# Transformer layer on one core: idle products behind the last products with v, the projection's column blocks in order 2, 3, 0, 1, and the paced DMA list served twice a unit

## The chip, the cores and the metric

The kernel runs on one core of a Trainium2 chip. The core has TensorE (PE in the profile; its weight loads are listed apart as PEld), VectorE (DVE), ScalarE (ACT), GpSimd (POOL) and SyncE (SP). Here SP's queue issues all the DMAs that matter. The metric is the device time of one execution in microseconds, lower being better.

## The reference

The layer normalises its input and adds an attention block and a feed-forward block to it:

```python
xn = layernorm(x)                      # x: 2048 x 512, float32
q, k, v = split(xn @ wqkv)             # 32 heads of 16
p = softmax(q @ k.T * 16 ** -0.5)      # per head 2048 x 2048
a = (p @ v) @ wo
h = gelu(xn @ w1 + b1) @ w2 + b2       # 512 -> 1792 -> 512
out = x + a + h
```

The kernel holds most float32 operands as a pair of float16 (high part and rest) and forms a product from three terms: high x high, high x rest, rest x high.

## The kernel before

**Units.** The heads are taken four at a time (8 groups g), the queries in 4 blocks of 512 (qb). A pair (g, qb) is a turn t, of which there are 32; a turn has 16 units, so there are 512. Unit u forms, for four heads, the scores whose row maxima are wanted (`s_half`: PE, then a maximum on DVE, L363). For the unit 19 before it (`LEAD`) it forms the transposed scores with the maximum taken off and their exponentials (`e_half`: PE, then ACT, L411), and for the units 20 and 21 before it the products with v (`v_half`), two halves a unit. A product uses 64 rows of the array and 32 columns; so PE runs two halves side by side, and beside each half of products with v it runs "dense" products on the other 64 rows, from a generator of groups: first the rest of v and the projections of q and k, then the feed-forward block, at last the output projection. `dense` takes 3 or 4 products of a group for each half.

**Order of the work.** Every engine's instructions are issued in the order in which the program writes them. `later(n, fn)` runs a function n slots on, a slot being the end of a unit (`tick`). A function with a size (`bulk`, in KB) is not run when it is due but goes to the end of the paced list (`lane`), from which `run_due` takes items while its credit is positive; the credit is raised by `LANE` once a unit and lowered by the item's size, and what is left of it is not kept. In the tick before every sixteenth unit the list is held (`held`), so that the store of a turn's maxima (L394) in that unit's first half goes ahead.

**First phase (`ph1`).** On the list are the stores of the normalised input (L1174), the loads of the weights for splitting (L812, `chunk`), the stores of the split weights (L1241, L1243), the stores of projected q and k (L592, L593) and the loads of the next group's q and k rows (`stacks`, L507). The weights for q and k come in four blocks of 128 columns; `load_qk(m + 1)` (L560) is called four slots after block m is split, and issues two loads of 256 KB directly. `split_qk` splits them with ACT (L149) and POOL (L151, L152), by the time project(m) begins; two buffers hold the loaded columns.

**After a turn.** `v_end` copies the four heads' sums from PSUM (L437). Through DRAM the sums of the exponentials are turned, inverted on DVE and spread over 128 partitions (`spread`, L463, four DMAs of 64 KB). POOL multiplies and splits, and L474 stores the turn's rows of the output projection's input (`ot_d`), after which the turn is in `ready`. For the last turn `last_one` does this on the chip instead: transposes on PE (L489), reciprocal and product on DVE (L491, L492), transposes back (L495), then the high part on ACT (L497) and the rest on DVE (L498).

**Tail.** `tail` yields the output projection's groups, by column block qb: 12 products on the lower 64 rows of the array and 12 on the upper. Blocks 2 and 3 are begun "early": they leave out the last 64 input rows (group 7's heads), which follow as `o_end` groups of three products on one side. `fetch(qb, n)` asks for a block's input (`oc`, L1361) n slots on. `when` lets it go once its turn is in `ready` and the unit number is in 4 to 13 of a sixteen, or past 512. The four pieces of the read and the reads of the accumulators (L1365) are on the list; `known` says that a block has been read. Block 3 needs turn 27, blocks 0 and 1 need turns 28 and 29, and the last rows of block 2 turn 30. Past unit 512 there are no scores, and `spare` puts products of a second group in their places, four a unit. `finish` adds the scaled product to the accumulator (L1371, DVE) and stores the result (L1368).

Of the kernel before, what the change touches and what calls it, by code (L numbers as in the profile page):

```python
# [36 lines left out]
WARM = 430  # L37
NV = 11
LAG, E_TAIL = 3000, 8000
LANE = 420  # L40
WFROM, WSTEP, XN = 10, 4.5, 4.5
VT = 2600, -2000
WV_TAIL, WV_DVE = 50000, 2
# [11 lines left out]
def layer_kernel(ctx: ExitStack, tc: tile.TileContext, x, wqkv, wo, w1, b1, w2, b2, out):  # L55
# [51 lines left out]
    def banks(tag):  # L107
        k = free_banks[tag].pop(0)
        free_banks[tag].append(k)
        return bank_tile(k, tag)  # L110
# [37 lines left out]
    def split_pool(hi, lo, src, inv):  # L148
        nc.scalar.activation(hi, src, AF.Copy, scale=inv)  # L149
        given("act", 1000)  # L150
        nc.gpsimd.tensor_scalar(src, src, inv, 0.0, op0=ALU.mult, op1=ALU.add)  # L151
        nc.gpsimd.tensor_tensor(lo, src, hi, op=ALU.subtract)  # L152
# [138 lines left out]
    def run_due(all_of_them=False):  # L291
        due = sorted((q for q in queue if q[0] <= slot[0]), key=lambda q: q[0])
        queue[:] = [q for q in queue if q[0] > slot[0]]
        for q in due:
            if q[3]:
                lane.append((q[3], q[1]))
            else:
                q[1]()
        credit[0] = min(credit[0], 0) + LANE
        while lane and (all_of_them or credit[0] > 0 and not held[0]):  # L300
            size, fn = lane.pop(0)
            credit[0] -= size
            fn()
# [123 lines left out]
    def v_end(u):  # L427

        t, kt = divmod(u, 16)
        g, qb = divmod(t, NQB)  # L430
        for h in range(4):
            del ptiles[u, h]
        if kt < 15:
            return
        pv, k = pv_of.pop(t)
        osb = work.tile([P, QB], F32, name="osb", bufs=2)
        nc.scalar.activation(osb, pv, AF.Copy)  # L437
        given("act", 600)
        free_banks["S"].append(k[0])
        if t == NG * NQB - 1:  # L440
            later(0, lambda: last_one(osb))
            return

        dn = work.tile([64, 32], F32, name="dn", bufs=1)
        rb = work.tile([P, QB], F32, name="rb", bufs=1)

        def sums():
            for h in range(4):
                nc.sync.dma_start(den_d[t, 0, h:h + 1, :], osb[32 * h + DH:32 * h + DH + 1, :])

        def turned():
            nc.sync.dma_start(dn, den_d[t, 0].rearrange("h (c q) -> (h c) q", q=32))

        def inverse():
            nc.vector.reciprocal(dn, dn)
            given("dve", 330)

        def keep():
            nc.sync.dma_start(den_d[t, 1].rearrange("h (c q) -> (h c) q", q=32), dn)

        def spread():
            for h in range(4):
                nc.sync.dma_start(rb[32 * h:32 * h + 32, :], den_d[t, 1, h:h + 1, :].to_broadcast([32, QB]))  # L463

        def store():
            ot = work.tile([P, 2, QB], F16, name="ot", bufs=2)
            pooled((1280, lambda: nc.gpsimd.tensor_tensor(osb, osb, rb, op=ALU.mult)),  # L467
                   (620, lambda: nc.gpsimd.tensor_scalar(ot[:, 0], osb, 1.0, 0.0, op0=ALU.mult, op1=ALU.add)),
                   (1160, lambda: nc.gpsimd.tensor_tensor(ot[:, 1], osb, ot[:, 0], op=ALU.subtract)),
                   (0, lambda: later(6 if t < (NG - 1) * NQB else 1, put)))  # L470

            def put():
                for h in range(4):
                    nc.sync.dma_start(ot_d[64 * g + DH * h:64 * g + DH * h + DH, :, qb * QB:(qb + 1) * QB],  # L474
                                      ot[32 * h:32 * h + DH])
                ready.add(t)


        at = (1, 3, 6, 7, 9, 12) if t < (NG - 1) * NQB else (1, 2, 5, 6, 7, 8)
        for k, fn in zip(at, (sums, turned, inverse, keep, spread, store)):  # L480
            later(k, fn)

    def last_one(osb):

        on = work.tile([P, 4, 4, DH], F32, name="on")
        rden = work.tile([P, 4, 4], F32, name="rden")
        pq = banks("S")
        for q in range(4):
            nc.tensor.transpose(pq[:, q * P:(q + 1) * P], osb[:, q * P:(q + 1) * P], ident)  # L489
        pqv = pq.rearrange("p (q h e) -> p q h e", q=4, h=4)  # L490
        nc.vector.reciprocal(rden, pqv[:, :, :, DH])  # L491
        nc.vector.tensor_tensor(on, pqv[:, :, :, 0:DH], rden.unsqueeze(3).to_broadcast([P, 4, 4, DH]), op=ALU.mult)  # L492
        pt = banks("S")
        for q in range(4):
            nc.tensor.transpose(pt[:64, q * P:(q + 1) * P], on[:, q].rearrange("p h d -> p (h d)"), ident)  # L495
        ot = work.tile([P, 2, QB], F16, name="ot", bufs=2)
        nc.scalar.activation(ot[:64, 0], pt[:64, :], AF.Copy)  # L497
        nc.vector.tensor_tensor(ot[:64, 1], pt[:64, :], ot[:64, 0], op=ALU.subtract)  # L498
        last.append(ot)
# [18 lines left out]
    class Group:  # L518
# [32 lines left out]
        def end(self):  # L551
            self.finish(self.bank)
            if self.key is not None:
                free_banks[self.key[1]].append(self.key[0])

    def load_qk(m):
        wf = []
        for w in range(2):
            wf.append(ph.tile([P, D], F32, name="wq", bufs=2).rearrange("p (c n) -> p c n", n=P))
            nc.sync.dma_start(wf[w], wqkv[:, w * D + m * P:w * D + (m + 1) * P].rearrange("(c p) n -> p c n", p=P))  # L560
        return wf

    def split_qk(m, wf, inv, ready_w):
        wh = ph.tile([P, 2, 2, NC, P], F16, name="wqk_h", bufs=2)
        for w in (1, 0):
            split_pool(wh[:, w, 0], wh[:, w, 1], wf[w], inv[:, 8 + 2 * min(m, 2) + w:9 + 2 * min(m, 2) + w])
            yield
        ready_w[m] = wh
        if m < 3:
            later(4, lambda: wfs.append(load_qk(m + 1)), True)  # L570
# [175 lines left out]
    def unit(gen):  # L746


        u = pos[0]
        e = u - LEAD  # L750
        if e > 0 and e % (2 * NQB * 16) == 0 and e < NU:
            fetch_scale(e // (2 * NQB * 16))
        pos[0] += 1
        for a in range(2):
            for kind, b in ((1, 1), (0, 0), (0, 1), (1, 0)) if a == 0 else ((1, 2), (0, 3), (0, 2), (1, 3)):
                if kind and 0 <= e < NU:
                    e_half(e, b)
                elif not kind and u < NU:
                    s_half(u, b)
                elif not kind and u > NU:  # L760
                    spare(gen, b % 2)
            if e >= 0:
                one_more()
                enter()

                w, r = (e - 2, 1) if a == 0 else (e - 1, 0)
                live = 0 <= w < NU
                new = r == 0 and w % 16 == 0
                if live and not new:
                    v_half(w, r)  # L770
                dense(gen, 1 - r)
                if live and new:
                    v_half(w, r)

                for user, goes_on in (("V", live and not (r == 1 and w % 16 == 15)),
                                      ("D", cur[0] is not None and not cur[0].over())):
                    leave(user, goes_on)
                for k in backlog:
                    backlog[k] = max(0, backlog[k] - HALF)
                if live and r == 1:  # L780
                    v_end(w)
                ended(False)

            if a == 0 and u % 16 == 0 and u // 16 - 1 in stores:
                stores.pop(u // 16 - 1)()
        if u < NU:
            s_end(u)
        tick()
# [626 lines left out]
    with ExitStack() as st3:  # L1415
# [17 lines left out]
                    later(n + 1 + k % 4, lambda k=k: read_acc(acs[k], k))  # L1433

        def tail():
            for n, qb in enumerate((2, 0, 3, 1)):
                fetch(qb, (2, 4, 10, 16)[n])
            later(9, lambda: nc.sync.dma_start(wo_l, wo_s[64:128, :, NC - 1, :]))
            ends = set()

            def rows():
                nc.sync.dma_start(ol, ot_d[D - 64:, :, 2 * QB:3 * QB])
                ends.add(2)

            when((NG - 1) * NQB + 2, rows)
            for qb in (2, 0, 3, 1):
                while qb not in known:
                    yield None
                for q in range(4):
                    yield o_proj(qb, q, qb >= 2)  # L1450
            while not ends:
                yield None
            for q in range(4):
                yield o_end(2, q, ol)
            while not last:
                yield None
            for q in range(4):
                yield o_end(3, q, last[0])
# [37 lines left out]
```

## Time and profile before

| | |
|---|---|
| median of 3 runs | 1469.63 us (1469.29 to 1471.78) |
| profiled execution | 1469.13 us |
| its span, first to last instruction | 1467.4 us |
| mean granted TensorE clock | 0.997 |
| busy: PE, DVE, ACT, POOL | 99%, 93%, 86%, 45% |
| data moved | 124.86 MB, 85 GB/s on average |

The span is the time from the first to the last instruction of the profiled execution; its own time is 1.7 us more. A chain of work is followed backwards from the last instruction to whatever released it, so its shares say what the span was made of. "Idle before" is the time for which an engine stood still ahead of an instruction, with what ended it; "issue" means that nothing in the profile explains the wait. A window's row gives its limits and its length, the busy time and count of what was asked for, the granted TensorE clock, the busy share of the DMA engines and GB/s. In a timeline the first number is the start and the second the length, in us from the start of the span.

### The profile page before, as it was taken

To read this page: it belongs to the slowest core of one execution; us is meant where nothing else is said; L and a number is where in the kernel's file an instruction comes from. 1 tells how busy PE (TensorE), PEld (TensorE's weight loads), DVE (VectorE), ACT (ScalarE), POOL (GpSimd) and SP (SyncE) were. 2 spreads that over 40 slices of the span, in tenths; PEclk is the share of its full clock that TensorE was granted. 3 is DMA by queue.
4 is the path that set the end of the run, shared out by engine and by line. 5 is a ranking of instruction groups with operands and counts; after the bars stand their busy time and mean duration, and the time that the engine had idled before them with its cause. 6 is when DMAs were issued, how large, how long until landed. Compare 5 with 4: busy or idle time off the path is not lost.

```text
span 1467.4 us, 88634 instructions
## 1 busy us (share of the span) xinstructions
PE 1451.0 (99%) x40158; PEld 839.5 (57%) x40158; DVE 1369.4 (93%) x2305; ACT 1258.4 (86%) x2366; POOL 663.9 (45%) x672
## 2 busy tenths in 40 slices
PE   8999999999999999999999999999999999999998
PEld 4446565665566555556565556565555656555554
DVE  7989999999999999999999999999999999999933
ACT  5868888888999888899988889998889998888884
POOL 3201957663778401288831138883115787121100
PEclk9999999999999999999999999999999999999999
DMA  6742465555224210221112111121112210111422
GB/s 211 221 127 64 151 193 176 162 163 157 82 60 130 67 35 25 65 67 41 45 44 88 30 37 44 52 76 45 44 38 76 55 37 22 56 56 33 142 94 96
DMA packets 112627, 124.86 MB, mean 85 GB/s; under 512 B 22908, under 2 KB 84220, under 8 KB 112248
## 3 DMA queue, kind: packets, MB, share of 16 engines
q1 hardware_dynamic: 112248, 119.18, 26.9%
q8 instruction: 314, 5.14, 1.5%
q14 instruction: 65, 0.53, 0.1%
HBM read 81.66 MB, written 37.34 MB: 81 GB/s over the span
## 4 chain that ended last, share of the span: by engine, by line
PE 95%; DVE 2%; DMA 1%; ACT 1%; issue 0%; SPq 0%; DVEq 0%; ACTq 0%
PE pV L169 27%; PE pD L169 27%; PE pT L169 20%; PE pS L169 18%; PE pT L993 1%; DVE mt L363 1%; PE pD L993 0%; DMA qk_d<-stg 0%; DMA wq<-in_A_wqkv_dram 0%; DVE ac L1371 0%; PE pT L963 0%; DMA kst<-qk_d 0%; DMA xs<-in_A_x_dram 0%; ACT xs L946 0%; DVE bs L931 0%
## 5 line engine op out<-in xcount | busy, mean ns | idle before, releaser
L363 DVE TENSOR_REDUCE mt<-pS 128x1 f32<-128x512 f32 x2029 | 1290.7, 683 | 35.8 <-PE pS L169 6.4
L411 ACT ACTIVATE pe<-pT 128x512 f32<-128x512 f32 x2048 | 1109.0, 599 | 161.8 <-PE pT L169 99.1
L169 PE MATMUL pV<-pe,vv 64*32 64x512 f32 x8192 | 1078.0, 595 | 0.1
L169 PE MATMUL pT<-qst,kst 64*32 64x512 f16 x8192 | 705.3, 377 | 1.0 <-issue 0.9
L169 PE MATMUL pS<-kst,qst 62*32 62x512 f16 x8116 | 588.4, 378 | 2.5 <-DVE mt L363 2.0
L169 PEld LDWEIGHTS <-qst 62*32 62x32 f16 x8192 | 292.0, 91 | 242.2 <-issue 44.8
L169 PE MATMUL pD<-xb,wc 64*32 64x512 f16 x5376 | 360.8, 376 | 0.0
L169 PE MATMUL pD<-w_s,g 64*32 64x512 f16 x5376 | 357.1, 377 | 0.0
L169 PEld LDWEIGHTS <-kst 64*32 64x32 f16 x8192 | 268.9, 91 | 111.5 <-issue 22.9
L169 PEld LDWEIGHTS pV<-pe,vv 64*32 64x32 f32 x8192 | 181.3, 105 | 84.7 <-PE pV L169 3.2
L169 PE MATMUL pD<-xt,wqk_h 64*32 64x512 f16 x2400 | 158.2, 377 | 0.2 <-issue 0.2
L169 PEld LDWEIGHTS <-wc 64*32 64x32 f16 x5376 | 123.5, 91 | 46.8 <-issue 0.6
L169 PEld LDWEIGHTS <-g 64*32 64x32 f16 x5376 | 118.1, 92 | 40.9 <-issue 0.2
L1338 POOL TENSOR_TENSOR xa<-xa,yt 128x512 f32<-128x512 f32 x16 | 20.5, 1283 | 226.9 <-ACT yt L1336 226.9
L467 POOL TENSOR_TENSOR osb<-osb,rb 128x512 f32<-128x512 f32 x31 | 39.9, 1287 | 164.6 <-DMA rb<-den_d 140.2
L1290 POOL TENSOR_TENSOR t<-hh 128x512 f32<-128x512 f32 x56 | 58.3, 1042 | 81.7 <-ACT hh L1313 80.5
L1285 POOL TENSOR_TENSOR t<-t,hh 128x512 f32<-128x512 f32 x56 | 71.9, 1284 | 4.7
L1292 POOL TENSOR_TENSOR t<-t,hh 128x512 f32<-128x512 f32 x56 | 71.8, 1283 | 4.7
L169 PEld LDWEIGHTS <-wqk_h 64*32 64x32 f16 x2400 | 57.2, 92 | 21.6 <-issue 2.9
L1287 POOL TENSOR_TENSOR g<-t,g 128x512 f16<-128x512 f32 x56 | 65.2, 1165 | 4.7
L1284 POOL TENSOR_SCALAR t<-t,gs 128x512 f32<-128x512 f32 x56 | 39.0, 696 | 58.4 <-ACT t L1279 58.3
L169 PE MATMUL pD<-wo_s,oc 64*32 64x512 f16 x828 | 54.5, 377 | 0.0
(164 smaller groups left out, 882.7 us busy)
## 6 DMA issues: line engine op xcount, KB each, us to landing
wc<-w_d SPq DMA_DIRECT2D x56, 256.0 KB
qk_d<-stg SPq DMA_DIRECT2D x32, 256.0 KB
rb<-den_d SPq DMA_DIRECT2D x124, 64.0 KB
wch<-in_B_w_dram SPq DMA_DIRECT2D x14, 512.0 KB
wch<-in_B_w_dram SPq DMA_DIRECT2D x28, 256.0 KB
w_d<-wsp SPq DMA_DIRECT2D x28, 256.0 KB
kst<-qk_d SPq DMA_DIRECT2D x64, 96.0 KB
qst<-qk_d SPq DMA_DIRECT2D x64, 96.0 KB
```

Source lines behind the costliest of these rows:

```text
L169: p = nc.tensor.matmul(*args, **kw)
L363: nc.vector.reduce_max(mt_of[t][:, n, qt, kb:kb + 1], s, axis=AX.X)
L411: nc.scalar.activation(pe, st, AF.Exp, scale=scale_of[g // 2])
L467: pooled((1280, lambda: nc.gpsimd.tensor_tensor(osb, osb, rb, op=ALU.mult)), (620, lambda: nc.gpsimd.tensor_scalar(ot[:, 0], osb, 1.0, 0.0 ...
L993: nc.tensor.matmul(tl[key], lhs, rhs, start=c + n == 0, stop=(c, n) == (NC - 1, 2))
L1284: pooled((690, lambda: nc.gpsimd.tensor_scalar(t1, t1, 1.0, gs[:, 1:2], op0=ALU.add, op1=ALU.mult)), (1280, lambda: nc.gpsimd.tensor_tenso ...
L1285: (1280, lambda: nc.gpsimd.tensor_tensor(t1, t1, hh, op=ALU.mult)),
L1287: (1160, lambda: nc.gpsimd.tensor_tensor(g[:, 1, f, :], t1, g[:, 0, f, :], op=ALU.subtract)),
L1290: pooled((1040, lambda: nc.gpsimd.tensor_tensor(t1, hh, hh, op=ALU.mult)), (620, lambda: nc.gpsimd.tensor_scalar(t1, t1, 1.0, 1.0 / GELU_A ...
L1292: (1280, lambda: nc.gpsimd.tensor_tensor(t1, t1, hh, op=ALU.mult)),
L1338: add = lambda: nc.gpsimd.tensor_tensor(xa, xa, yt, op=ALU.add)
```

## The change

Three things are changed. Eight products of 128 x 512 whose result nobody reads go onto PE in `last_one`: three before the first transposes, three before the second, two after them. The output projection takes its column blocks in the order 2, 3, 0, 1, and asks for their inputs 2, 1, 10 and 14 slots after the tail begins. The list is served once in the middle of each unit and once at its end, with a credit of 225 each time; the spread of the reciprocals takes 256 off the credit; and the loads of the columns of q and k go onto the list.

```diff
-LANE = 420
+LANE = 225
...
+        run_lane(all_of_them)
+
+    def run_lane(all_of_them=False):
         credit[0] = min(credit[0], 0) + LANE
         while lane and (all_of_them or credit[0] > 0 and not held[0]):
...
         def spread():
             for h in range(4):
                 nc.sync.dma_start(rb[32 * h:32 * h + 32, :], den_d[t, 1, h:h + 1, :].to_broadcast([32, QB]))
+            credit[0] = min(credit[0], 0) - 256
...
+    def idle(n):
+        wp = banks("T")
+        for _ in range(n):
+            nc.tensor.matmul(wp, wo_s[:, 0, 0, 0:P], wo_s[:, 0, 0, :], start=True, stop=True)
+
     def last_one(osb):
 
+        idle(3)
         on = work.tile([P, 4, 4, DH], F32, name="on")
...
         nc.vector.tensor_tensor(on, pqv[:, :, :, 0:DH], rden.unsqueeze(3).to_broadcast([P, 4, 4, DH]), op=ALU.mult)
+        idle(3)
         pt = banks("S")
         for q in range(4):
             nc.tensor.transpose(pt[:64, q * P:(q + 1) * P], on[:, q].rearrange("p h d -> p (h d)"), ident)
+        idle(2)
...
+    here = {(1, 0), (1, 1)}
+
     def load_qk(m):
         wf = []
         for w in range(2):
             wf.append(ph.tile([P, D], F32, name="wq", bufs=2).rearrange("p (c n) -> p c n", n=P))
-            nc.sync.dma_start(wf[w], wqkv[:, w * D + m * P:w * D + (m + 1) * P].rearrange("(c p) n -> p c n", p=P))
+
+            def load(w=w):
+                nc.sync.dma_start(wf[w], wqkv[:, w * D + m * P:w * D + (m + 1) * P].rearrange("(c p) n -> p c n", p=P))
+                here.add((m, w))
+
+            later(0, load, True, 256)
         return wf
...
+            if a == 0:
+                run_lane()
             if a == 0 and u % 16 == 0 and u // 16 - 1 in stores:
                 stores.pop(u // 16 - 1)()
...
-            for n, qb in enumerate((2, 0, 3, 1)):
-                fetch(qb, (2, 4, 10, 16)[n])
+            for n, qb in enumerate((2, 3, 0, 1)):
+                fetch(qb, (2, 1, 10, 14)[n])
...
-            for qb in (2, 0, 3, 1):
+            for qb in (2, 3, 0, 1):
```

More of the change, by code (lines that the diff above doesn't have):

```diff
@@ L565, in split_qk @@
         for w in (1, 0):
+            assert (m, w) in here
             split_pool(wh[:, w, 0], wh[:, w, 1], wf[w], inv[:, 8 + 2 * min(m, 2) + w:9 + 2 * min(m, 2) + w])
```

## The prediction

> **What bounds the kernel now.** I read the page first, then the count of exponentials by stretch (four per unit, so a clock of the unit loop), then the waits and SP's queue where that clock runs slow, and last the chain that ended last.
>
> ```profile
> span 1467.4 us, 88634 instructions
> PE 1451.0 (99%) x40158; PEld 839.5 (57%) x40158; DVE 1369.4 (93%) x2305; ACT 1258.4 (86%) x2366; POOL 663.9 (45%) x672
> q8 instruction: 314, 5.14, 1.5%
> PE 95%; DVE 2%; DMA 1%; ACT 1%; issue 0%; SPq 0%; DVEq 0%; ACTq 0%
> ```
>
> PE is busy throughout and carries 95% of the chain that ended last; DVE follows closely. So a change wins only by making units shorter or by shortening the end, where PE is no longer full.
>
> The next rows are the exponentials' windows (start and end, length, ACT busy and count, clock, DMA share, GB/s). Each holds 64 of them and the first of the next unit: 16 units.
>
> ```profile
> 140.20:184.40 44.20, 34.80 (x65) 1.00 0.54 164
> 227.80:272.40 44.60, 34.91 (x65) 1.00 0.51 168
> 315.50:357.70 42.20, 34.59 (x65) 1.00 0.59 182
> 1239.40:1281.70 42.30, 34.78 (x65) 1.00 0.15 40
> ```
>
> Sixteen units take 42.3 us late in the run at the pace of four dense products a half, and up to 44.6 us in the first phase. So the first phase loses about 2 us in each of the two slow windows shown. That is where the paced list works.
>
> **Where the first phase loses.** SP's timeline (start, length), PE's, one of SP's waits (total, times, longest), then ACT's:
>
> ```profile
> 94.65 0.59 SPq L1174 DMA_DIRECT2D xn_d<-xt  x1
> 118.47 2.93 SPq L560 DMA_DIRECT2D wq<-in_A_wqkv_dram  x2
> 133.75 1.22 SPq L394 DMA_DIRECT2D m_d<-mhl  x2
> 137.64 1.19 SPq L345 DMA_DIRECT2D qst<-m_d  x4
> 138.87 0.78 SPq L507 DMA_DIRECT2D kst<-qk_d  x2
> 139.70 2.76 SPq L812 DMA_DIRECT2D wch<-in_B_w_dram  x4
> ...
> 164.08 1.06 SPq L560 DMA_DIRECT2D wq<-in_A_wqkv_dram  x2
> ...
> 166.38 2.75 SPq L463 DMA_DIRECT2D rb<-den_d  x4
> 169.22 0.38 SPq L592 DMA_DIRECT2D qk_d<-stg  x1
> ```
>
> ```profile
> 170.30 0.39 PE L169 MATMUL pT<-qst,kst 64*32 64x512 f16 x3 [0.86 <-issue]
> ```
>
> ```profile
> SPq L560 <- POOL wqk_h L152: 2.1, 1, 2.1
> ```
>
> ```profile
> 150.33 0.72 ACT L149 ACTIVATE wqk_h<-wq,inv 128x512 f16<-128x512 f32 x1
> ```
>
> SP runs ahead of PE until something tied to PE holds it: a maxima store (L394), a reciprocal. Then it issues all it has in one burst. At 169.4 PE waited 0.86 us for nothing the profile shows, right after the q and k columns of 164.08 and the spread of the reciprocals (L463, 64 KB each) had gone out together. PE's program itself comes by DMA (314 packets of q8, 5.14 MB, 16 KB each), so I read this stall as a late block of program behind a burst. That reading is an inference: the row names only "issue".
>
> **The change, part by part.**
>
> *The columns of q and k.* They leave SP's direct order and join the list. For column block 2 the slot is one later, which falls behind the held unit: the maxima store of 133.75 now comes first. SP no longer stands at L560 from 95.2 to 118.5, but then it stands at L394 instead, so nothing else starts earlier. After 137.64 the list holds, in this order, one pair of kst loads (192), four wch halves (4 x 256), then the two wq loads. At 225 a service they go out within four units. On SP that is 138.87 + 0.78 + 2.76 + 2 x 0.5 (the pair at 164.08 took 1.06), so about 143.5. ACT needs them at 150.33, so 6 us remain for landing. Cost: 0, hidden by those 6 us. If they land later, ACT stands with the exponentials behind it and PE follows, 1 us for 1 us. Moving 512 KB from the quiet 118 us into the burst is a loss for the program fetch, bounded by one more stall of 0.86 us. Block 3's loads wait for POOL's split of block 2 to free their buffers; that held SP 2.1 us at 162, and a slot in the list later it holds it no longer, with the q and k stores and chunks queued behind it.
>
> *Twice a unit, 225 for 420.* The rate goes from 15 x 420 = 6300 KB in 16 units to 30 x 225 - 256 = 6494 KB. SP reaches one waiting instruction from the last in a burst either way, so serving at half units only interleaves. The pause of 256 at the spread does act on time: about one 256 KB item less in the three units behind L463, which is where the stall above lies. Bounds: all the excess of the two shown windows gone, 44.2 + 44.6 - 2 x 42.3 = -4.2 us; or two more stalls of 0.86 us, +1.7. I take one stall of 0.86 us gone: -0.9, nearest to the only row that names a stall.
>
> On the rule of the Trainium skill: "Runtime: NRT & Kernel Launch", section "Instruction fetch mechanics", says that PE's program streams in 16 KiB blocks fetched ahead and that crossing a block is mostly hidden. The block size agrees with 5.14 MB over 314 packets; "hidden" does not fit an 0.86 us issue wait, unless that has another cause. By the page this term would be 0 and the sum 0.9 us later.
>
> *The order 2, 3, 0, 1.* Rows of the output projection's products (PE busy and count; POOL's is zero) and of the exponentials, then SP:
>
> ```profile
> 1366.30:1374.40 8.10, 5.60 (x88) 0.00 (x0) 1.00 0.64 193
> 1376.90:1383.93 7.03, 0.05 (x4) 0.00 (x0) 1.00 0.61 179
> 1400.20:1450.40 50.20, 48.71 (x852) 0.00 (x0) 1.00 0.24 77
> ```
>
> ```profile
> 1411.00:1450.00 39.00, 32.28 (x60) 1.00 0.19 62
> ```
>
> ```profile
> 1331.15 3.27 SPq L474 DMA_DIRECT2D ot_d<-ot  x4
> ...
> 1354.16 2.79 SPq L474 DMA_DIRECT2D ot_d<-ot  x4
> ...
> 1367.91 0.58 SPq L1361 DMA_DIRECT2D oc<-ot_d  x1
> ```
>
> Block 2's four groups end at about 1376.9; then three units, 7.03 us, have no dense product, because block 0 waits for the rows put at 1354.16, and `when` may then read only in units 4 to 13 of a sixteen: 1367.91. Block 3 (without its last 64 rows) needs only the rows put at 1331.15, so its reads go out from unit 493 in place of 500 and the three units are filled. They then cost what a filled unit costs: 39.00/15 = 2.60 us each against 7.03/3 = 2.34, so +0.8 us. The 3 x 8 half-products done there are missing later, where twelve a unit are done (8 dense and 4 in the places of the scores): the work ends two units sooner. Walked by hand, three units a dense group and six a spare one, block 1 follows at about unit 521 with its rows known at 518, and the last two units hold only the last-rows groups of block 2. At 2.34 for 2.60 they give back 0.5.
>
> *The end.* The chain that ended last (start, length), and DVE's and ACT's timelines:
>
> ```profile
> 1454.22 1.04 PE pD L169 x16
> 1455.26 0.60 PE pS L489 x4
> ...
> 1456.18 0.43 DVE on L492
> 1456.61 0.14 issue
> 1456.75 0.61 PE pS L495 x4
> ...
> 1458.06 0.68 DVE ot L498
> ```
>
> ```profile
> 1454.09 0.60 ACT L437 ACTIVATE osb<-pV 128x512 f32<-128x512 f32 x1 [3.99 <-issue]
> ...
> ```
>
> ```profile
> 1458.67 0.73 DVE L1371 SCALAR_TENSOR_TENSOR ac<-pD,gs,ac 128x512 f32<-128x512 f32 x1
> 1459.33 0.73 DVE L1371 SCALAR_TENSOR_TENSOR ac<-pS,gs,ac 128x512 f32<-128x512 f32 x1
> 1459.98 4.02 DVE L1371 SCALAR_TENSOR_TENSOR ac<-pD,gs,ac 128x512 f32<-128x512 f32 x6
> ```
>
> The first transposes wait behind 16 left-over products until 1455.2, though osb is done at 1454.69. With the left-over gone they can start 0.14 us behind it (as the second ones stand behind DVE), 1454.83: -0.4. Behind `ot`, DVE has eight adds, 0.66 us apart: block 1's last, three of block 2's last rows, four of block 3's. By the walk five remain: 3 x 0.66 = -2.0. What is late next is PE, with three products a group, and the stores behind the last add, so I take no more than that.
>
> *Idle products.* Eight of 128x512. Sixteen tiles' products of the left-over took 1.04 us, so four full ones about the same: 0.26 each. Three stand beside ACT's copy (0.60) and reach 0.2 us past it at most; three stand beside DVE's reciprocal and product (1455.9 to 1456.6, 0.7), two beside ACT and DVE (1457.4 to 1458.7). Cost 0, up to +0.3 if the first three outlast the copy. The clock they might guard is not falling here:
>
> ```profile
> 1456.00:1458.00 2.00, 1.25 (x13) 0.59 (x14) 0.56 (x2) 0.59 (x1) 0.00 (x0) 1.00 0.03 8
> 1462.00:1464.00 2.00, 0.23 (x2) 0.00 (x0) 2.00 (x4) 0.00 (x0) 0.00 (x0) 1.00 1.00 380
> ```
>
> With PE busy 1.25 of 2 us the granted clock is 1.00, and still 1.00 when PE has stopped. Gain 0.
>
> **Sum**, against the profiled execution's 1469.13 us: -0.9 + 0.8 - 0.5 - 0.4 - 2.0 = -3.0, so 1466.1; the runs' median, 1469.63, stands 0.5 above that execution, so I forecast 1466.4.
>
> **The rivals.**
> *Only the end moves.* The list's term is zero, because SP bursts as before. Then -2.1: 1467.3 to 1467.5. For it: SP's rows show bursts set by waits, not by the list. Against it: the stall lies just behind the spread.
> *The filled units cost what the end gives.* If filled units cost as the slowest first-phase pace (44.60/16 = 2.79) and the end keeps seven of its eight adds, +1.35 - 0.4 - 0.7: no change, 1469.4.
> *Slower.* The wq loads of block 2, now behind six others in the burst, land after ACT's 150.33; ACT holds four exponentials a unit behind the split, and PE the products with v. From 1 us of lateness it eats the list's term, from 5 us (landing at 155.3) the time is above 1469.6, and from 8 us it is over 0.2% slower: 1472.6. Against it: 6 us of room.
> By the Trainium skill's page above, the first of these would be the forecast.
>
> **How the numbers follow.** 0.2%, 2.9 us, is about what a measurement of this kernel can tell from no change. Forecast 0.48 (all of it faster or at that bound: 1463 to 1466.7); only the end 0.27 and cost eats gain 0.10, together 0.37 within 0.2%; slower 0.15. Lower end: the bound -4.2 in place of -0.9 gives 1463; upper end: between no change and the slower rival, 1470.8, leaving about 0.2 outside. The likeliest case alone: 1464.5 to 1466.8.
>
> **What would show it.** No L560 before 133.75, and the first split at 150.33 unmoved. The window at 140 us shorter than 44.2 us, and no issue wait behind the first spread. No empty units between block 2 and the next block, and products of block 3 in them. No 16 left-over products ahead of the transposes; five adds behind `ot` instead of eight. The forecast is wrong if the first-phase windows keep or grow their 44 us, if ACT waits for wq, or if the last units hold as much as before.

## The result and the profile after

| | before | changed |
|---|---|---|
| median of 21 runs on one chip | 1470.01 us (1468.95 to 1473.84) | 1468.02 us (1465.71 to 1471.52) |
| ratio of the runs, 95% interval | 1 | 0.9984 [0.9977, 0.9991] |
| profiled execution, own time | 1469.13 us | 1471.52 us |

The ratio says 2.4 us less, between 1.3 and 3.4: faster, and less than the 0.2% (2.9 us) that the prediction named as its bound. The profiled execution of the changed kernel is the slowest of its 21 runs, so the two spans can't be set against each other. I compare stretches instead, and take two more executions of the same changed kernel beside it (called c_full and c_full2 below).

The page of the changed kernel, its span, its busy times and its chain by engine:

```profile
span 1469.7 us, 88685 instructions
PE 1451.6 (99%) x40184; PEld 838.7 (57%) x40184; DVE 1368.7 (93%) x2304; ACT 1259.3 (86%) x2367; POOL 664.1 (45%) x673
...
PE 95%; DVE 2%; ACT 1%; DMA 1%; issue 1%; SPq 0%; DVEq 0%; ACTq 0%
```

The shares are those of before; "issue" has gone from 0% to 1%. PE has 26 products more, eight of which are the idle ones; matmul records can be missing, so the other 18 say nothing. All that there is to see lies in three places.

**The first phase.** SP's timeline of the changed kernel (start, length), where the prediction had the wq loads at 143.5:

```profile
133.58 1.21 SPq L397 DMA_DIRECT2D m_d<-mhl  x2
137.45 1.14 SPq L348 DMA_DIRECT2D qst<-m_d  x4
138.63 0.78 SPq L519 DMA_DIRECT2D kst<-qk_d  x2
139.45 2.62 SPq L834 DMA_DIRECT2D wch<-in_B_w_dram  x4
142.17 0.96 SPq L576 DMA_DIRECT2D wq<-in_A_wqkv_dram  x2
```

The order is the one walked by hand: the maxima store, the kst pair, four halves of wch, the two loads of wq. They end at 143.13. ACT never waited for them: the first split came at 151.23, after an issue wait of 1.19 us of PE's weight loads at 148.5.

Windows of the exponentials in the changed kernel, the same stretches of 16 units as in the prediction (window, length, ACT busy and count, clock, DMA share, GB/s):

```profile
139.50:184.60 45.10, 35.07 (x65) 1.00 0.54 161
228.80:272.30 43.50, 34.72 (x65) 1.00 0.51 166
316.30:359.30 43.00, 34.46 (x65) 1.00 0.59 184
```

45.1, 43.5 and 43.0 us, against 44.2, 44.6 and 42.2 before: one shorter, two longer. The sum over the whole first phase, 96 units, in one execution of the kernel before and in two of the changed one (the first two rows below are before and changed, the third is c_full):

```profile
95.00:357.70 262.70, 208.59 (x385) 1.00 0.47 145
```

```profile
94.80:359.80 265.00, 208.93 (x385) 1.00 0.46 144
```

```profile
93.70:356.40 262.70, 208.76 (x385) 1.00 0.46 145
```

c_full2, the third execution of the changed kernel, took 261.5. One kernel so takes 261.5 to 265.0 us for the same 96 units, with the one execution of before in the middle. In this phase a single pair of profiles decides nothing below 3.5 us.

**The tail.** The last 32 units of the changed kernel (exponentials, as above; the second row ends with the first exponential of the last unit):

```profile
1368.80:1412.60 43.80, 34.61 (x65) 1.00 0.40 121
1412.60:1453.00 40.40, 32.77 (x61) 1.00 0.22 72
```

and its output projection's products (PE busy and count; those that read the weights `wo_s`, and so without the groups of the last rows) in two windows:

```profile
1379.70:1388.70 9.00, 5.60 (x84) 0.00 (x0) 0.00 (x0) 1.00 0.55 174
1452.90:1459.00 6.10, 1.07 (x21) 0.07 (x2) 0.00 (x0) 1.00 0.43 165
```

The 7 us in which the kernel before had 0.05 us of dense work are gone: the 9 us at 1379.7 are filled like any others, with 84 products. In the last 6 us there are 21, one of them an idle product, and no block of 16 left-over ones stands behind the last product with v any more.

**The end.** The chain that ended last in the changed kernel (start, length), then DVE's and PE's timelines (in brackets the idle time ahead of the instruction, and what ended it):

```profile
1458.58 0.59 PE pV L169 x2
...
1462.57 0.69 DVE ot L510
...
1463.32 0.40 PE pD L554
1463.74 0.67 DVE ac L1393
```

```profile
1463.74 2.78 DVE L1393 SCALAR_TENSOR_TENSOR ac<-pD,gs,ac 128x512 f32<-128x512 f32 x4 [0.48 <-PE pD L554]
```

```profile
1458.93 0.82 PE L490 MATMUL pT<-wo_s 128*128 128x512 f16 x3
1459.77 0.66 PE L499 MATMUL pS<-ident,osb 128*128 128x128 f32 x4
1460.26 0.81 PE L490 MATMUL pT<-wo_s 128*128 128x512 f16 x3
1461.23 0.63 PE L506 MATMUL pS<-ident,on 128*64 128x128 f32 x4 [0.16 <-DVE on L502]
1461.69 0.59 PE L490 MATMUL pT<-wo_s 128*128 128x512 f16 x2
1463.32 2.33 PE L554 MATMUL pD<-wo_l,ot 64*128 64x512 f16 x10 [0.17 <-DVE ot L510]
```

L490 are the idle products. The first transposes start at 1459.77, 1.36 us behind the start of the last product with v; before it was 1.81. Behind `ot` four adds remain of eight, and the last ends at 1466.52. From the start of the last product with v to the end of the last add it is 8.12 us; in the kernel before 10.63. The clock at this end (window, length, then busy and count of PE, PEld, DVE, ACT, POOL, then the clock):

```profile
1460.00:1462.00 2.00, 1.84 (x13) 1.00 (x11) 0.69 (x3) 0.10 (x1) 0.00 (x0) 1.00 0.64 235
1462.00:1464.00 2.00, 1.57 (x8) 0.43 (x7) 0.94 (x2) 0.49 (x1) 0.00 (x0) 1.00 0.03 12
1464.00:1466.00 2.00, 1.64 (x8) 0.54 (x6) 2.00 (x4) 0.00 (x0) 0.00 (x0) 1.00 0.31 121
```

The clock is full as long as PE works, as predicted. That this needs the idle products is seen below.

### The profile page after: what moved, and what is told of

The parts are those of the page before. It is cut to its first block, busy times and chain, and to the rows that moved or that the text cites. A ratio compares the mean times of both kernels' runs of the same rounds, so it can differ in the third digit from the quotient of the medians.

```text
span 1469.7 us, 88685 instructions
## 1 busy us (share of the span) xinstructions
PE 1451.6 (99%) x40184; PEld 838.7 (57%) x40184; DVE 1368.7 (93%) x2304; ACT 1259.3 (86%) x2367; POOL 664.1 (45%) x673
## 4 chain that ended last, share of the span: by engine, by line
PE 95%; DVE 2%; ACT 1%; DMA 1%; issue 1%; SPq 0%; DVEq 0%; ACTq 0%
PE pV L169 28%; PE pD L169 27%; PE pT L169 20%; PE pS L169 18%; PE pT L1015 2%; DMA wq<-in_A_wqkv_dram 1%; DVE mt L366 1%; PE pD L1015 1%; ACT xs L968 0%; ACT pe L414 0%; DVE ac L1393 0%; ACT wqk_h L904 0%; DVE xt L998 0%; DMA out_dram<-ac 0%; PE pT L985 0%
```

## The experiments

Three stretches are compared throughout, all in us and each from one profiled execution: the first phase (96 units), the last 32 units (from their first exponential to the start of the last product with v) and the end (start of the last product with v to end of the last add). Beside them stands the ratio of the runs to the kernel before, measured on the same chip. The 368 units behind the first phase took 966.6 to 968.6 us in every kernel but one (told below), without order; the 16 after those took 42.0 in each.

| kernel | ratio, 95% interval | first phase | last 32 units | end |
|---|---|---|---|---|
| before | 1 | 262.8 | 87.2 | 10.63 |
| changed | 0.9984 [0.9977, 0.9991] | 265.0 | 89.2 | 8.12 |
| c_full | 0.9987 [0.9978, 0.9996] | 262.7 | 89.0 | 8.12 |
| c_full2 | 0.9984 [0.9974, 0.9994] | 261.5 | 87.8 | 8.12 |
| e1_order | 0.9993 [0.9984, 1.0002] | 263.1 | 88.2 | 10.14 |
| e2_idle | 1.0002 [0.9993, 1.0011] | 262.4 | 87.2 | 11.23 |
| e3_list | 0.9998 [0.9989, 1.0007] | 263.9 | 88.0 | 10.98 |
| e8_no_idle | 0.9997 [0.9988, 1.0006] | 264.9 | 88.0 | 9.25 |
| e4_order_idle | 0.9980 [0.9971, 0.9990] | 264.6 | 88.6 | 8.11 |
| e11_paced | 0.9983 [0.9973, 0.9993] | 262.7 | 87.6 | 8.12 |
| e12_paced2 | 0.9976 [0.9967, 0.9985] | 260.3 | 88.5 | 8.12 |
| e14_paced3 | 0.9972 [0.9961, 0.9982] | 261.1 | 88.0 | 8.12 |

My theory, from the prediction: the end gives most, the list a little, the idle products nothing. The rivals: only the end moves; or the list is what matters; or a part costs what another gives.

### One part at a time

**The order alone** (e1_order), against the kernel before:

```diff
-            for n, qb in enumerate((2, 0, 3, 1)):
-                fetch(qb, (2, 4, 10, 16)[n])
+            for n, qb in enumerate((2, 3, 0, 1)):
+                fetch(qb, (2, 1, 10, 14)[n])
...
-            for qb in (2, 0, 3, 1):
+            for qb in (2, 3, 0, 1):
```

> The kernel before with the order 2, 3, 0, 1 and its fetch offsets alone. My theory: this is the part that moves the end. The three units without dense products are filled (+0.8 us), the last units hold less (-0.5), the 16 left-over products ahead of the transposes are gone (-0.4), and five adds stand behind ot instead of eight (-2.0): -2.1 us, ratio 0.9986. The span from the last product with v to the last add falls from 10.7 us to about 8.2. Rival one (the list carries the change): ratio 1.000, because the filled units cost what the end gives. Rival two (the idle products carry it): ratio 1.000 as well, and the end shortens only where they stand.

0.9993 [0.9984, 1.0002], and the end at 10.14, not near 8. The reason stands in the clock's column of its windows:

```profile
1458.00:1460.00 2.00, 1.32 (x6) 0.28 (x5) 0.68 (x1) 0.59 (x1) 0.00 (x0) 0.80 0.08 27
1460.00:1462.00 2.00, 2.00 (x6) 0.71 (x5) 0.99 (x2) 0.00 (x0) 0.00 (x0) 0.50 0.00 0
```

At about 1459.2, 4.35 us behind the start of the last product with v, the granted clock falls to half, and the last products run at it: six in 2 us of full business. Four adds stand behind `ot`, one fewer than walked, but each now waits for PE, and the clock took most of the gain back.

**The idle products alone** (e2_idle), against the kernel before:

```diff
+    def idle(n):
+        wp = banks("T")
+        for _ in range(n):
+            nc.tensor.matmul(wp, wo_s[:, 0, 0, 0:P], wo_s[:, 0, 0, :], start=True, stop=True)
...
     def last_one(osb):
...
+        idle(3)
...
         nc.vector.tensor_tensor(on, pqv[:, :, :, 0:DH], rden.unsqueeze(3).to_broadcast([P, 4, 4, DH]), op=ALU.mult)
+        idle(3)
         pt = banks("S")
...
+        idle(2)
         ot = work.tile([P, 2, QB], F16, name="ot", bufs=2)
```

> The kernel before with the eight idle products alone. My theory: three of them now stand between the 16 left-over products and the first transposes, with nothing to hide behind, because osb is done before them: 3 x 0.22 to 0.26 us, +0.7 us, ratio 1.0005; the other five stay beside DVE and ACT. The granted clock is 1.00 there with and without them. Rival (they keep TensorE ready): the matmuls behind them get shorter and the time falls by up to 0.5 us, ratio 0.9997.

1.0002 [0.9993, 1.0011]; the end 11.23, that is 0.6 longer. Its chain that ended last (start, length):

```profile
1453.06 1.04 PE pD L169 x16
1454.10 0.75 PE pT L486 x3
1454.85 0.45 PE pS L495 x4
```

With the left-over products still there, the three idle ones (L486) stand ahead of the transposes (L495) on the path itself: the first transposes come 2.47 us behind the last start of a product with v in place of 1.81, and the end moves by as much. Here the idle products guard nothing and cost their time.

**The list alone** (e3_list): LANE 225 with a second service a unit, the pause of 256 at the spread, and the loads of wq on the list, with the kernel before's order and no idle products:

```diff
-LANE = 420
+LANE = 225
...
+            credit[0] = min(credit[0], 0) - 256
...
+            later(0, load, True, 256)
...
+            if a == 0:
+                run_lane()
```

> The kernel before with everything on the list alone: served twice a unit at 225, 256 off at the spread, the columns of q and k on it. My theory: one stall of 0.9 us less in the first phase, ratio 0.9994, with the 16-unit windows of the first phase still 43 to 45 us. Rival one (the list carries the change): -2 us, ratio 0.9986, first-phase windows at or below 43 us. Rival two (SP bursts as before): 1.0000.

0.9998 [0.9989, 1.0007], the first phase 263.9 against 262.8. Nothing gained, nothing lost that can be told. The parts of the list were not tried one by one.

**All but the idle products** (e8_no_idle): the changed kernel with the three calls of `idle` taken out.

```diff
-        idle(3)
...
-        idle(3)
...
-        idle(2)
```

> The changed kernel without the eight idle products. My theory: they cost nothing and gain nothing there, so this is the changed kernel's time, ratio 0.9984 to the kernel before (at most 0.0002 lower, if the first three outlast ACT's copy). Rival (they keep TensorE ready): 0.5 us slower than the changed kernel, 0.9988.

0.9997 [0.9988, 1.0006]; the end 9.25 against 8.12. Windows at the end, as above, and PE's last products:

```profile
1458.00:1460.00 2.00, 1.17 (x8) 0.67 (x8) 0.81 (x3) 0.00 (x0) 0.00 (x0) 1.00 0.71 256
1460.00:1462.00 2.00, 1.16 (x5) 0.41 (x6) 0.82 (x2) 0.59 (x1) 0.00 (x0) 1.00 0.04 15
1462.00:1464.00 2.00, 2.00 (x8) 0.69 (x6) 1.59 (x3) 0.00 (x0) 0.00 (x0) 0.60 0.26 99
```

```profile
1461.44 3.55 PE L546 MATMUL pD<-wo_l,ot 64*128 64x512 f16 x10 [0.17 <-DVE ot L502]
```

PE is busy 1.17 and 1.16 us of two times 2, and then the clock goes to half, at 1462.4. The last ten products take 3.55 us, where the changed kernel needs 2.33. In e1_order and here the end runs alike up to the first last-row product, 4.13 us behind the start of the last product with v. Then the clock falls 4.35 us behind that start in one and 5.87 in the other, and so the end is 10.14 long in one and 9.25 in the other. With the idle products it is 8.11 and 8.12. They buy 2.0 and 1.1 us in these two profiles, one execution each; the moment of the fall makes the difference, not the list (more on it in the last section).

**Order and idle products, the list as before** (e4_order_idle): the diffs of e1_order and e2_idle together. It ran with c_full, the changed kernel once more, on one chip.

> The kernel before with the new order and the idle products, and with the list as it was. If the end carries the whole change (new theory): as the changed kernel, 0.9984 to 0.9990, the last add 8.1 us behind the last product with v and the clock whole until it. If the list carries 0.9 us of it (the prediction): 0.9 us slower than the changed kernel, ratio 0.9990 to 0.9994.

> The changed kernel as it is, beside the others of this call on one chip. New theory: at the end the order's shorter DVE queue and the idle products work together (order 2, 3, 0, 1 leaves TensorE with so little to do behind the last product with v that its granted clock is halved, and the idle products keep it whole): ratio 0.9984 to 0.9988, and 8.1 us from the last product with v to the last add. Old theory (the idle products give nothing): the same here as without them, 0.9993.

0.9980 [0.9971, 0.9990] without the list's changes, 0.9987 [0.9978, 0.9996] with them. Either part alone shows no difference that can be told (0.9993, 1.0002); together they carry the whole change, and the list adds nothing to it that can be told. The order without the idle products stands at 0.9993 and 0.9997, with them at 0.9980 and 0.9984: 1.9 us in both pairs, though the intervals of each pair overlap.

The table says the same of the list in the first phase, where it was to work. The five profiles with the list's changes (changed, c_full, c_full2, e3_list, e8_no_idle) took 263.6 us on average, the four with the list as before (before, e1_order, e2_idle, e4_order_idle) 263.2.

### The stall that the list was to remove

The prediction read the 0.86 us issue wait behind the first spread as a late block of PE's program behind a burst of DMAs. That was an inference. The DMA records of the traces bear it out. In the 14 traces of this case there are 68 waits of PE or of its weight loads, after the first 100 us, that are put down to "issue" and last 0.7 us or more. In 67 of them work goes on 1.2 to 1.6 us after a 16 KB packet of q8, the queue that carries the program, has ended, though such packets come only every 4.4 us; for the 0.86 us of the prediction it is 1.54. What makes the blocks late is the next question.

Two kernels put traffic into the middle of the run, where the kernel before moves little. Both leave nothing out; the copies go to a place that is not read.

**Short bursts** (e9_burst): behind the spread of 16 turns, eight copies of 256 KB at once.

```diff
+            if 8 <= t < 24:
+                for k in range(8):
+                    nc.sync.dma_start(junk_d[k], wo_s[:, 0, 0:2, :])
```

> The kernel before with eight DMAs of 256 KB more, from SBUF to DRAM that nobody reads, behind the spread of the reciprocals in each of the turns 8 to 23, a stretch in which sixteen units take 41.6 to 42.4 us and hardly a stall is seen. If bursts make PE's program late: 16 more bursts of 2 MB, each with no, one or two stalls of about 1 us, 5 to 20 us longer, with issue waits of PE just behind the spreads. If not: the same within 1 us.

1.0004 [0.9994, 1.0014]. Nothing that can be told. A burst shows like this (6 us, PE busy 6.00, DMA share 0.79, 283 GB/s), and PE stays full through it:

```profile
675.00:681.00 6.00, 6.00 (x180) 3.57 (x176) 6.00 (x11) 5.56 (x11) 3.84 (x5) 1.00 0.79 283
```

**Steady traffic** (e13_traffic): two copies of 256 KB in most units from 150 to 399.

```diff
+    def traffic(k):
+        if 150 <= pos[0] < 400 and pos[0] % 16 not in (14, 15, 0, 1):
+            if k:
+                nc.sync.dma_start(junk_d[pos[0] % 4], wo_s[:, 0, 0:2, :])
+            else:
+                nc.sync.dma_start(junk_d[4 + pos[0] % 4], xn_d[:, :, pos[0] % 4, 0:QB])
```

> The kernel before with two more DMAs of 256 KB a unit (one from SBUF to DRAM, one from DRAM to DRAM, read by nobody) in units 150 to 399, outside the ends of the turns: about the first phase's traffic in a stretch that is quiet. If steady traffic of that size makes PE's program late: issue waits of 0.4 to 1.3 us as in the first phase, and 8 to 16 us longer over these 250 units. If the first phase's stalls have another cause: within 2 us.

1.0272 [1.0253, 1.0292]: 40 us more, where 8 to 16 were expected, all in the middle (1007.7 us for the 368 units, against 966.6). The same 650 us in the kernel before and in this one (all engines, then clock, DMA share, GB/s):

```profile
450.00:1100.00 650.00, 649.35 (x18972) 381.49 (x18964) 639.08 (x1054) 575.57 (x1083) 292.73 (x297) 1.00 0.19 53
```

```profile
450.00:1100.00 650.00, 628.70 (x17824) 359.44 (x17822) 602.91 (x991) 544.47 (x1022) 288.69 (x292) 1.00 0.61 192
```

and the waits of PE's weight loads and of PE in that stretch (total, times, longest), first before, then with the traffic:

```profile
PEld L169 <- issue: 21.8, 95, 0.5
```

```profile
PEld L170 <- issue: 59.4, 158, 2.5
PE pT L170 <- issue: 5.9, 9, 2.1
PE pD L170 <- issue: 5.4, 7, 1.3
PE pT L170 <- DMA qst<-m_d: 4.1, 4, 1.6
```

Most of the added waits are issue waits, that is, PE waited for nothing that the profile names, up to 2.5 us at a time. A smaller part is late data, which shows as a wait for a DMA: four waits of PE, 4.1 us together, for the maxima rows (qst). The long issue waits here, 0.7 us or more, end 1.27 to 1.61 us after a packet of the program's queue. That this traffic brings the issue waits is shown; that they are waits for late blocks of program is what the packets say, and no row of the profile names it. Traffic that lasts did it (DMA share 0.61), bursts of 6 us (0.79) didn't. But the two differ in kind as well: half of the lasting copies read from DRAM, those of the bursts all read from SBUF, and length and kind were not tried apart. The first phase of this kernel, at 0.46 to 0.59, has lasting traffic and stalls behind the same packets. By the Trainium skill ("Runtime: NRT & Kernel Launch", section "Instruction fetch mechanics") crossing a block of program is mostly hidden. In the quiet middle the trace agrees (longest wait 0.5 us), under this traffic it doesn't.

**Spreading the traffic** (e11_paced): if SP's running ahead makes the issue waits, they should fall when SP is held back by something that moves with PE. In units 31 to 111 of the changed kernel, SP copies 4 bytes of the unit's maxima to a place nobody reads, and so waits for DVE.

```diff
+        u = pos[0] - 1
+        if LEAD + 12 <= u < 112:
...
+            nc.sync.dma_start(pace_d[u:u + 1, :], mt_of[t][0:1, 3, qt, kb:kb + 1])
```

> The changed kernel with one more DMA of 4 bytes a unit in the first phase, from the maxima that DVE has just written, so that SP cannot run ahead of PE and the list is served in the units' own time and not in bursts behind a wait. If the first phase's stalls are late blocks of PE's program behind bursts of DMA: the six first-phase stretches fall from 263 to 265 us to 257 to 260, ratio 0.994 to 0.997 to the kernel before, and the issue waits of 0.9 us are gone. If they have another cause: the stretches as they were, and the 80 DMAs more cost nothing or delay loads (ratio 0.998 to 1.002).

0.9983 [0.9973, 0.9993], no better than the change. The waits from 100 to 360 us, first in the kernel before, then here:

```profile
PEld L169 <- issue: 12.9, 48, 1.4
```

```profile
PEld L170 <- issue: 9.6, 43, 0.7
...
PE pT L170 <- DMA qst<-m_d: 1.4, 2, 1.1
...
PEld L170 <- DMA qst<-m_d: 2.4, 2, 1.6
```

The longest issue wait is halved, and the wait of the weight loads for the maxima rows (qst) has grown from 0.5 us in total to 2.4. They are read back behind the list's traffic, which now reaches into the turn's end; that this is the reason is argued, and the next kernel tries it.

**Holding the list at the end of a turn** (e12_paced2): e11's copies stay, up to unit 107, but the list stands still, and no copy is made, in a turn's last two units, with 270 a service to make up for it; the inputs of the tail are asked for later as well.

```diff
-LANE = 225
+LANE = 270
...
-        held[0] = pos[0] < NU and pos[0] % 16 == 0
+        held[0] = pos[0] < NU and pos[0] % 16 in ((14, 15, 0) if pos[0] < 112 else (0,))
...
-                fetch(qb, (2, 1, 10, 14)[n])
+                fetch(qb, (2, 1, 16, 20)[n])
```

> The paced kernel (4 bytes a unit tie SP to DVE's maxima in the first phase), with the list held in the last two units of a turn as well, at 270 a service, so that the store of the maxima finds the DMA queues quiet; and blocks 0 and 1 asked for 16 and 20 slots on, so that block 0's reads do not meet the others at 1370 to 1380 us. Theory: the paced kernel lost its gain to the maxima's rows, which came late (3.8 us of PE's waits on them), and not to program blocks: now the first-phase stretches sum to 259 to 261 us and the 30th turn takes 42.4 to 42.8 us; ratio 0.996 to 0.998. Rival (the list's bursts cost nothing): first phase 262 to 265 us as before, ratio 0.998 to 0.999.

0.9976 [0.9967, 0.9985]. The first phase took 260.3 us, the shortest seen, and both waits are small:

```profile
PEld L170 <- issue: 8.8, 40, 0.5
PEld L170 <- DMA qst<-m_d: 0.4, 1, 0.4
```

The last 32 units took 88.5, inside the 87.8 to 89.2 of the changed kernel, with one unit of 3.46 us at a DMA share of 0.93: asking later in the tail shows no gain.

**The best of both** (e14_paced3): e12's hold and its 270 in the first phase alone, the changed kernel's tail. It ran with c_full2 on one chip.

```diff
-        credit[0] = min(credit[0], 0) + LANE
+        credit[0] = min(credit[0], 0) + (270 if pos[0] < 112 else LANE)
```

> The paced kernel with the list held at the ends of the turns, at 270 a service in the first phase alone, and with the changed kernel's own fetch offsets and 225 in the tail, where the offsets of 16 and 20 cost one unit of 3.46 us. Theory: 260 to 261 us in the first phase and 40.1 us in the last turn's row, so 2 to 3 us faster than the changed kernel: ratio 0.996 to 0.9975. Rival (the 260 us were one execution's luck): as the changed kernel, 0.998 to 0.999.

> The changed kernel once more, beside the next one on the same chip: ratio 0.998 to 0.999 to the kernel before, 262 to 265 us in the six first-phase stretches.

0.9972 [0.9961, 0.9982] against 0.9984 [0.9974, 0.9994]: 1466.04 us. It is the fastest kernel here and faster than before by 2.6 to 5.7 us. That it beats the change is likely and not settled: the intervals overlap, though of the 88 pairs of one run of each, e14_paced3 is the faster in 74. Its first phase, 261.1 us, is only 0.4 below the changed kernel's best (261.5). The long stalls speak for the pacing: between 100 and 360 us the profiles without the 4-byte copies have one to four issue waits of 0.7 us or more, those of e11_paced, e12_paced2 and e14_paced3 none, none and one.

## Why the prediction was right, and where it was not

The forecast was 1466.4 us, 3.2 less than the median before. Measured on one chip, the change is worth 2.4 (1.3 to 3.4). That is inside the range, and it lies nearer to the rival "only the end moves" (2.1) than to the forecast; the interval holds both. The sum itself gives 3.0 less and so 1466.6; the other 0.2 of the forecast has no reason in it. The total came out well because its largest terms, those of the end, had the right size; but the reason given for them was incomplete, and two smaller terms (-0.9 and -0.5) did not show. Part of that is luck: by the prediction's reasoning the order alone was to shorten the end, and the order alone does it by 0.5 us and not 2.4. The idle products, taken for nothing, happened to be in the same change.

**The end: right in both sizes, for the new order with the idle products.** Transposes: predicted -0.4, measured 1.81 to 1.36, -0.45. Adds behind `ot`: predicted eight to five, -2.0; from the end of `ot` to the end of the last add it was 5.27 and is 3.27, -2.0. There are four behind `ot`, not five; the time between ends fell by what I said because PE with three products a group is late next, as named: the first add waits 0.48 us for PE.

**The idle products at 0: wrong, the step that failed worst.** I read the clock off the kernel before, where PE is at 1.25 of 2 us and the clock stays at 1.00, and took that for proof that nothing is to be guarded. But that reading holds for one window of 2 us, with the 16 left-over products just ahead of it; and another part of the same change takes these away. Without the idle products the new order leaves PE at 1.17 and 1.16 of 2 us in two windows running in e8_no_idle, and in both kernels without them the clock is halved while last-row products are still to come. With them it is not. They are worth 1.1 and 2.0 us of the 2.5 at the end in the two profiles, and cost 0.6, where I had bounded the cost at 0.3, only where the left-over is still there (e2_idle). So the -2.0 for the adds was not the order's alone.

**The list at -0.9: no run shows it.** e3_list gave 0.9998, an interval that still holds -0.9. But e4_order_idle, without the list's changes, came out at 0.9980 where the whole change had 0.9984 to 0.9987, and the first phase is 0.4 us longer on average with the list's changes, not 0.9 shorter, though the single profiles scatter by more. The stalls did not go either: of issue waits of 0.7 us or more between 100 and 360 us the kernel before has three and the changed kernel four, two and one in its three profiles. My own rival has a reason that fits: SP's bursts are set by the waits that release it, and serving twice a unit only interleaves them. The late block of program was read rightly; the price was wrong, since I took one stall from one execution for it. The same kernel's first phase varies by 3.5 us from execution to execution, so a stall at one place is no term. Here the Trainium skill's page cited in the prediction would have given the better number, 0, though its reason, that the crossing is hidden, does not hold in this traffic.

**The columns of q and k at 0: right.** The SP order is the one walked, and ACT didn't wait. The slower rival did not occur.

**The filled units at +0.8: right, with a stall on top.** The 16 units there went from 41.9 to 42.6 in e8_no_idle and to 42.7 in c_full2. In the changed kernel's own execution, in c_full and in e4_order_idle one unit more was 0.8 to 1.1 us long (43.5 to 43.8). The block's reads now go out earlier, in a stretch with the DMAs busy 0.40 to 0.55. It is the same kind of stall: in that unit PE's weight loads wait 1.19, 0.91 and 0.91 us for "issue" in the three profiles, and go on 1.29 to 1.44 us after a packet of the program's queue.

**The last two units at -0.5: wrong, it is about 0.** The last 15 units grew from 39.7 to 40.0 to 40.4, and the rest up to the last product with v shrank from 5.6 to 5.1. The walk found the empty units at the very end, and missed that the third unit of an early group, which has 16 dense products in place of 24, is now in an earlier stretch, so that those of the last 15 are all full. That is a reading of products by unit; no run isolates it.

**The sum by the traces**: the end -2.5, the units ahead of it +0.6 (c_full2, no stall) to +2.0 (with one). So -1.9 to -0.5, where the runs say -2.4 (-1.3 to -3.4). The rest of the unit loop scatters by more than this difference from one execution to the next, so I can't divide it further.

## What to carry to other kernels

A reading of the clock, or of any cover, belongs to the schedule it was read in: where one part of a change takes work away from just ahead of it, the reading has to be made again for what is left, and two parts that each do nothing alone can carry the gain together. Before a stall is priced, look for it in a second execution; if the stretch scatters by more than the stall, it is a bound and not a term. A pace in program order is lost as soon as the queue runs ahead; tying the queue to an engine that does the work, and holding it ahead of reads that others wait for, gave the shortest first phases here (260.3 and 261.1 us), with a gain in the runs that is likely and not settled.

## What was not expected of the hardware

The clock was halved though PE never stood still for long. In e8_no_idle its waits behind the last products with v were 0.77, 0.81 and 0.68 us, with transposes of 0.6 us between them, and PE was busy 58% of 4 us; then the granted clock went to 0.50 for the rest. The Trainium skill ("TensorE: Matmul & The Clock Gate", section "What's actually happening") ties half clock to an idle window of about 3.4 us. The length agrees with these traces: the long stretch at full clock lasts 1443.84, 1447.25, 1450.66, 1454.08 or (e13_traffic) 1491.62 us in the 14 of them, and these lie 3.41 us, or a whole number of times that, apart. So the clock changes only at the ends of such intervals, and where they lie is another matter in every execution: in three profiles of the changed kernel it fell 7.77, 10.58 and 10.11 us behind the start of the last product with v.

That the interval must be idle does not agree. These are the intervals of 3.41 us at whose end the clock stayed (before, first row) or fell (e1_order, e8_no_idle, changed), with PE's busy time first:

```profile
1454.01:1457.43 3.42, 2.50 (x32) 1.24 (x31) 0.68 (x2) 0.65 (x2) 0.00 (x0) 1.00 0.21 79
1455.79:1459.20 3.41, 1.49 (x9) 0.89 (x10) 1.52 (x4) 0.97 (x2) 0.00 (x0) 1.00 0.59 212
1458.98:1462.40 3.42, 2.19 (x11) 0.95 (x12) 1.54 (x3) 0.59 (x1) 0.00 (x0) 1.00 0.23 84
1462.77:1466.18 3.41, 2.70 (x12) 0.86 (x10) 2.93 (x5) 0.00 (x0) 0.00 (x0) 1.00 0.23 88
```

It stayed at 73% and fell at 44, 64 and 79%. (In the changed kernel the fall came 0.5 us after PE's last product and cost nothing.) So PE's busy share alone does not tell whether the clock will fall. A rival is that the kind of work counts: the first three intervals hold transposes, the last only products on half of the array's rows. No run here settles what counts. What is shown is that eight products of 0.27 us held the clock up until PE had done its work in all seven profiles that have them behind the new order.

Bursts at a DMA share of 0.79 for 6 us cost nothing that could be told; 0.61 for hundreds of microseconds, with copies of another kind among them, cost 40 us of 967, while the issue waits of PE's weight loads rose from 21.8 to 59.4 us in 650 us.
